# Attention, then two expert layers: six more tiles transposed by TensorE instead of by DMA

## The chip, the cores and the metric

The kernel runs on one core of one Trainium2 chip. The metric is the device time of one execution in microseconds, as the median of several runs. Five engines work side by side, each on its own queue of instructions in a fixed order: TensorE (PE; its weight loads are listed as PEld), VectorE (DVE), ScalarE (ACT), GpSimd (POOL) and SyncE (SP), which issues the transfers.

## The reference

```python
scores = np.matmul(q, k.transpose(0, 1, 3, 2)) / np.sqrt(D)   # q, k, v: 4 x 8 x 576 x 64
rel = np.abs(pos[:, None] - pos[None, :])
x = np.log1p(rel) / np.log1p(np.maximum(pos[:, None], 1.0))
bias = np.maximum(x[..., None] @ w1 + b1, 0.0) @ w2           # 32 hidden, 8 heads
scores = scores + bias.transpose(2, 0, 1)
attn = exp(scores - max) / (sum + 1e-9)
x = (attn @ v) as 2304 tokens x 512
h = max(x @ moe_w1, x @ moe_w2, x @ moe_w3)                   # 768 wide
x = h @ moe_w_out                                             # 512 wide
h = x @ moe2_w_in                                             # 2048 wide
g = h where h >= 1, 0 where h <= -1, else (h + 1)**2 / 4
out = g @ moe2_w_out
```

All arrays are float32. The kernel multiplies most matrices as pairs of float16 parts, a high and a low one, with three products for each pair of operands.

## The kernel before

The queries of a batch are cut into four blocks of 128 (j = 0 to 3) and a rest of 64. A **unit** is one block of one batch. The rest, called SJ (j = 4), packs two heads into one tile, so its unit has 4 **slots** where a long unit has 8, one for each head. Blocks 0 to 2 run over all four batches; then, batch by batch, block 3 and the rest follow, so the last two units are block 3 and the rest of batch 3: 8 and 4 slots, the last 12 of 144.

A slot goes like this. TensorE computes the scores in float32 (L632, in a PSUM tile s); VectorE adds the bias and takes the maximum (L644); ScalarE takes the exponential and its sum (L646), which leaves the tile pf (of the pool `sp`, 4 buffers). For the product with v (**PV**, L682 in the rest, L686 elsewhere), pf must be transposed and split into float16 parts. In most slots ScalarE writes the high part (L662), GpSimd the low part (L663 and L664) into a tile phl, and SyncE issues one DMA transpose (L666) of both into a tile pt (4 buffers). In every second slot of block 0 (j = 0) it is done otherwise: TensorE turns pf in float32 against an identity matrix (L651 four times 128 columns, L652 the last 64) into two tiles of the PSUM pool pm, ScalarE copies the high part out (L655, L656) and VectorE subtracts it for the low part (L657, L658). No DMA takes part. This is called a **set** below.

The pool pm has three buffers. They serve these sets, the products of the first layer (L741, 12 matmuls to a group) and of the second (L763, 18 to a group), and the small products that find the scale of a weight (L447). Groups are emptied by ScalarE (L746, L768) or VectorE (L748).

After the PV of a unit, VectorE divides by the sums (L698), ScalarE and GpSimd split (L700, L701), and a DMA transpose (L709) brings it to xT, which the first layer multiplies (L741), from work that is queued while later slots run. The first layer's result is split again (L752, L753) before L763, and L768 and L770 bring the result to DRAM.

Beside it run the **late pieces**, the 32 weight pieces of the last layers. Each is loaded (L416) in two 32-bit words, decoded by ScalarE (L428, L429) and VectorE (L430, L431), its scale found by L447, and split (L156, L157). Some land in the buffers of the tile v: two buffers, which also hold the v of a unit and half its heads, loaded by L601. When the last L741 and L763 are done, the last stage starts, which alternates L969 and L993.

What order each engine's instructions get is set by a scheduler that simulates times while the kernel is built; on the chip the order is fixed, and an instruction that waits holds up all behind it on its engine. This is true of SyncE's queue of transfers too.

```python
for j, b in [(j, b) for j in range(3) for b in range(B)] + [(j, b) for b in range(B) for j in (3, SJ)]:
```

Of the kernel before, what the change touches and what calls it, by code (L numbers as in the profile page):

```python
# [20 lines left out]
def kernel(ctx: ExitStack, tc: tile.TileContext, qt, kt, vr, small, mw1, mw2, mw3, mwo, win, wo2, out):  # L21
# [9 lines left out]
    B, H, S, D = 4, 8, 576, 64  # L31
# [60 lines left out]
    def st(shape, dt, tag):  # L92
        return sb.tile(shape, dt, tag=tag, name=tag, bufs=BUFS.get(tag, 1))
# [69 lines left out]
    if True:  # L163
# [61 lines left out]
        def mlp_ps():  # L225
            return ps.tile([P, 512], F32, tag="pm", name="pm", bufs=3)
# [343 lines left out]
        for j, b in [(j, b) for j in range(3) for b in range(B)] + [(j, b) for b in range(B) for j in (3, SJ)]:  # L570
            u = Unit()
# [62 lines left out]
        def halves(t):  # L634
            return t.rearrange("p (a c) -> p a c", a=2)

        def emit_soft(i):
            u, s = slots[i]
            if s == 0:
                u.sums = st([P, H], F32, "sums")  # L640
            h = s if u.j == SJ else HEADS[s]
            sn = st([P, S], F32, "sp")
            mx = st([P, 1], F32, "mx")
            V.tensor_tensor_reduce(halves(sn), sbox.pop(i)[:, :, :288], halves(bias_sb[u.j][:, h]), -0.125, 3e38, ALU.add, ALU.min, mx)  # L644
            pf = sn
            A.activation(pf, sn, AF.Exp, scale=-1.0, bias=mx, accum_out=u.sums[:, h:h + 1])  # L646
            if u.j == 0 and s % 2:

                pa, pe = mlp_ps(), mlp_ps()[0:64, :P]
                for c in range(4):  # L650
                    T.transpose(pa[:, P * c:P * c + P], pf[:, P * c:P * c + P], ident)  # L651
                T.transpose(pe, pf[:, 512:], ident)  # L652
                pt = st([P, 9, P], F16, "pt")
                pa = pa.rearrange("p (c i) -> p c i", c=4)
                A.activation(pt[:, 0:4], pa, AF.Copy)  # L655
                A.activation(pt[0:64, 4], pe, AF.Copy)  # L656
                V.tensor_tensor(pt[:, 5:9], pa, pt[:, 0:4], ALU.subtract)  # L657
                V.tensor_tensor(pt[64:128, 4], pe, pt[0:64, 4], ALU.subtract)  # L658
                ptbox[i] = pt
                return  # L660
            hl = st([P, 2 * S], F16, "phl")
            A.activation(hl[:, :S], pf, AF.Copy)  # L662
            G.tensor_tensor(hl[:, S:S + 64], pf[:, 512:], hl[:, 512:S], ALU.subtract)  # L663
            G.tensor_tensor(hl[:, S + 64:], pf[:, :512], hl[:, :512], ALU.subtract)  # L664
            pt = st([P, 9, P], F16, "pt")
            SP.dma_start_transpose(out=pt, in_=hl)  # L666
            ptbox[i] = pt
# [192 lines left out]
        for i in range(NS + LAG + 1):  # L860
            if i < NS:
                u, s = slots[i]
                at = i - start_of[u.j]
                if at == 0 and u.j < 3:
                    with behind(i):
                        new_xt(u.j + 1)
                    bias_q.extend((u.j + 1, gq) for gq in range(18))
                    if u.j == 2:
                        bias_q.extend((SJ, gq) for gq in range(9))
                with sooner("att"):  # L870
                    prefetch(i + PRM["ahead"])
                    prefetch_v(i)
                    emit_s(i + 1)
                    emit_soft(i)
# [199 lines left out]
```

## Time and profile before

| | |
|---|---|
| time, median of 3 runs | 1066.14 us (1061.78 to 1069.17) |
| the profiled execution | 1069.84 us, span 1068.1 us |
| TensorE busy | 969.3 us (91%) |
| VectorE busy | 688.4 us (64%) |
| ScalarE busy | 543.8 us (51%) |
| GpSimd busy | 310.2 us (29%) |
| mean granted clock of TensorE | 0.936 of full |
| the last scores L632 start | 575.0 us |

The page is of one execution, seen by the hardware profiler; its span is the time from the first to the last instruction. Busy shares are means over stages with different limits: TensorE is nearly full in most slices, while in the slices around 580 to 600 us it isn't. So the stretch from 545 to 600 us, in which the last twelve slots run, has to be read by itself.

### The profile page before, as it was taken

The numbers are of one execution on the slowest core, as the hardware profiler recorded it, in microseconds if no ns is written. First come the engines' busy times: TensorE is split into PE (matmuls) and PEld (weight loads), VectorE is DVE, ScalarE is ACT, GpSimd is POOL, SyncE is SP. The second block draws the span as 40 slices with busy tenths as digits, with TensorE's granted clock in tenths as the row PEclk, the third lists the DMA queues.
The fourth block names the chain that finished last, engine by engine and source line by source line (L and its number), as shares of the span: only waits on it lengthen the run. The fifth ranks groups of instructions, "written<-read, shape, count | busy, mean of one in ns | idle before, by whom it ended". The sixth has DMA issues, their size and how long they took to land.

```text
span 1068.1 us, 23316 instructions
## 1 busy us (share of the span) xinstructions
PE 969.3 (91%) x9218; PEld 671.4 (63%) x9218; DVE 688.4 (64%) x1614; ACT 543.8 (51%) x1104; POOL 310.2 (29%) x425
## 2 busy tenths in 40 slices
PE   6687879799999989999897788999999999999994
PEld 5555667678888878777686677644444444444562
DVE  8979877886555677456565598876654464454452
ACT  4486555676665645666666466543232332332341
POOL 1132234577767755556565112000000000000000
PEclk8676779899999989999999899999999999999997
DMA  9696767499999898989887745010110100000010
GB/s 299 198 284 172 181 152 159 119 216 201 241 231 210 188 181 156 192 218 224 186 180 182 211 153 164 21 40 1 40 40 1 40 21 1 7 34 1 4 38 20
DMA packets 229425, 138.94 MB, mean 130 GB/s; under 512 B 177988, under 2 KB 208196, under 8 KB 228804
## 3 DMA queue, kind: packets, MB, share of 16 engines
q1 hardware_dynamic: 229316, 137.45, 53.9%
q8 instruction: 72, 1.18, 0.5%
q14 instruction: 37, 0.30, 0.1%
HBM read 79.68 MB, written 15.27 MB: 89 GB/s over the span
## 4 chain that ended last, share of the span: by engine, by line
PE 63%; DMA 12%; DVE 12%; ACT 4%; issue 4%; SPq 2%; POOL 1%; DVEq 0%; POOLq 0%; ACTq 0%
PE pm L969 17%; PE s L993 17%; PE pm L741 11%; PE s L632 7%; PE pm L763 3%; PE pav L686 3%; DMA ws<-in_moe_w_out_dram 3%; DMA ws<-in_moe_w_in_dram 2%; PE pm L367 2%; DMA pt<-phl 2%; DVE sp L644 2%; DMA v<-in_moe_w_in_dram 2%; DMA aw<-in_moe_w_dram 1%; DVE aw L430 1%; DVE aw L157 1%
## 5 line engine op out<-in xcount | busy, mean ns | idle before, releaser
L741 PE MATMUL pm<-xT,aw 128*128 128x256 f16 (+1 forms) x2160 | 247.9, 268 | 19.6 <-ACT hm L746 4.9
L741 PEld LDWEIGHTS <-aw 128*128 128x128 f16 x2160 | 192.5, 100 | 59.9 <-issue 32.4
L664 POOL TENSOR_TENSOR phl<-sp,phl 128x512 f16<-128x512 f32 x128 | 154.2, 1205 | 0.1
L646 ACT ACTIVATE sp<-sp,mx 128x576 f32<-128x576 f32 x144 | 110.6, 769 | 84.1 <-DVE mx L644 83.8
L632 PE MATMUL s<-k,qz 64*128 64x288 f32 (+1 forms) x576 | 140.1, 475 | 10.6 <-DVE mx L644 9.7
L993 PEld LDWEIGHTS <-phl 128*128 128x128 f16 x864 | 84.5, 98 | 98.3 <-DVE phl L985 0.2
L981 DVE SCALAR_TENSOR_TENSOR sp<-pm,vec,sp 128x512 f32<-128x512 f32 (+1 forms) x80 | 55.8, 697 | 112.7 <-ACT sp L980 112.7
L980 ACT ACTIVATE sp<-pm,vec 128x512 f32<-128x512 f32 (+1 forms) x80 | 58.7, 733 | 123.8 <-PE pm L969 122.2
L993 PE MATMUL s<-ab,phl 128*128 128x512 f16 x486 | 112.5, 379 | 0.0
L984 ACT ACTIVATE phl<-sp,vec 128x512 f16<-128x512 f32 (+1 forms) x80 | 54.3, 678 | 109.4 <-DVE sp L982 109.4
L663 POOL TENSOR_TENSOR phl<-sp,phl 128x64 f16<-128x64 f32 x128 | 47.0, 367 | 205.9 <-ACT phl L662 152.6
L644 DVE CUSTOM_DVE_ANT_0 sp<-s,ab 128x576 f32<-128x576 f32 x128 | 93.1, 750 | 17.2 <-PE s L632 11.5
L632 PEld LDWEIGHTS s<-k,qz 64*128 64x128 f32 (+1 forms) x576 | 76.7, 207 | 36.4 <-DVE mx L644 13.9
L985 DVE SCALAR_TENSOR_TENSOR phl<-sp,vec,phl 128x512 f16<-128x512 f32 (+1 forms) x80 | 55.8, 698 | 51.7 <-ACT phl L984 51.6
L969 PEld LDWEIGHTS <-ab 128*128 128x128 f16 x540 | 52.7, 98 | 53.6
L686 PEld LDWEIGHTS <-pt 128*128 128x128 f16 x1792 | 73.5, 100 | 19.5 <-issue 7.8
L662 ACT ACTIVATE phl<-sp 128x576 f16<-128x576 f32 x128 | 84.0, 673 | 1.2 <-DMA pt<-phl 0.5
L763 PE MATMUL pm<-hh,wo 128*128 128x256 f16 x648 | 78.3, 276 | 5.7 <-ACT hh L752 3.5
L686 PE MATMUL pav<-v,pt 128*128 128x64 f16 x1568 | 70.3, 196 | 6.1 <-ACT pt L655 3.5
L763 PEld LDWEIGHTS <-wo 128*128 128x128 f16 x648 | 62.4, 99 | 13.4 <-issue 4.9
L753 POOL TENSOR_TENSOR hh<-hm,hh 128x256 f16<-128x256 f32 (+1 forms) x60 | 43.7, 728 | 92.5 <-ACT hh L752 92.5
L748 DVE SCALAR_TENSOR_TENSOR hm<-pm,hm 128x256 f32<-128x256 f32 (+1 forms) x120 | 46.9, 391 | 34.7 <-ACT hm L746 20.3
(213 smaller groups left out, 1445.8 us busy)
## 6 DMA issues: line engine op xcount, KB each, us to landing
k<-in_k_dram SPq DMA_DIRECT2D x64, 288.0 KB, 4.2
v<-v_d SPq DMA_DIRECT2D x24, 640.0 KB, 4.9
ws<-in_moe_w_out_dram SPq DMA_DIRECT2D x14, 512.0 KB, 4.5
x_d<-hl SPq DMA_DIRECT2D x36, 128.0 KB, 2.6
qz<-in_q_dram SPq DMA_DIRECT2D x16, 256.0 KB, 4.6
ab<-in_moe_w_dram SPq DMA_DIRECT2D x8, 512.0 KB, 8.5
ws<-in_moe_w_in_dram SPq DMA_DIRECT2D x8, 512.0 KB, 4.1
v<-in_moe_w_out_dram SPq DMA_DIRECT2D x8, 512.0 KB, 3.7
```

Source lines behind the costliest of these rows:

```text
L632: T.matmul(sbox[i + r][:, c, :288], q[p, s if u.j == SJ else s // 2], k[p, 288 * c:288 * c + 288], start=True, stop=True)
L644: V.tensor_tensor_reduce(halves(sn), sbox.pop(i)[:, :, :288], halves(bias_sb[u.j][:, h]), -0.125, 3e38, ALU.add, ALU.min, mx)
L646: A.activation(pf, sn, AF.Exp, scale=-1.0, bias=mx, accum_out=u.sums[:, h:h + 1])
L662: A.activation(hl[:, :S], pf, AF.Copy)
L664: G.tensor_tensor(hl[:, S + 64:], pf[:, :512], hl[:, :512], ALU.subtract)
L686: T.matmul(u.pav[:, 64 * h:64 * h + 64], pt[:, c], v[:, sl, 64 * (h % 4):64 * (h % 4) + 64], **kw)
L741: T.matmul(o, wm[:, ft, i, wp, kk], x_rhs(key, xp, kk) if n == 256 else x_rhs(key, xp, kk)[:, c], start=(x == 0), stop=(x == 11))
L763: T.matmul(pm, wo16[:, ft, wp, P * d:P * d + P], hh[:, ft, hp], start=(ft == 0 and y == 0), stop=(ft == NF1 - 1 and y == 2))
L969: T.matmul(pm, w[:, wp, kk], x2t[j][:, kk, xp], start=(x == 0), stop=(x == 11))
L980: A.activation(r, pm, AF.Relu, scale=c_ch[:, f], bias=c_half)
L981: V.scalar_tensor_tensor(t, pm, c_c[:, f], r, ALU.mult, ALU.max)
L993: T.matmul(acc[c], gl[:, n * gp + P * c:n * gp + P * c + P], w[:, wp], start=(start and y == 0), stop=(stop and y == 2))
```

## The change

The condition under which a slot takes the set of L651 to L658 in place of L662 to L666 is widened: from every second slot of block 0 to every second slot of the last two units also. These are the slots 1, 3, 5 and 7 of block 3 and 1 and 3 of the rest, in batch 3.

```diff
-            if u.j == 0 and s % 2:
+            if (u.j == 0 and s % 2) or (u.j >= 3 and u.b == B - 1 and s % 2):
 
                 pa, pe = mlp_ps(), mlp_ps()[0:64, :P]
                 for c in range(4):
                     T.transpose(pa[:, P * c:P * c + P], pf[:, P * c:P * c + P], ident)
                 T.transpose(pe, pf[:, 512:], ident)
                 pt = st([P, 9, P], F16, "pt")
                 pa = pa.rearrange("p (c i) -> p c i", c=4)
                 A.activation(pt[:, 0:4], pa, AF.Copy)
                 A.activation(pt[0:64, 4], pe, AF.Copy)
                 V.tensor_tensor(pt[:, 5:9], pa, pt[:, 0:4], ALU.subtract)
                 V.tensor_tensor(pt[64:128, 4], pe, pt[0:64, 4], ALU.subtract)
                 ptbox[i] = pt
                 return
             hl = st([P, 2 * S], F16, "phl")
             A.activation(hl[:, :S], pf, AF.Copy)
             G.tensor_tensor(hl[:, S:S + 64], pf[:, 512:], hl[:, 512:S], ALU.subtract)
             G.tensor_tensor(hl[:, S + 64:], pf[:, :512], hl[:, :512], ALU.subtract)
             pt = st([P, 9, P], F16, "pt")
             SP.dma_start_transpose(out=pt, in_=hl)
```

The scheduler then orders the stretch anew on every engine. On SyncE, before, this stood from the last late pieces that are loaded during the attention to the first one behind it. pt is a tile for PV, xT the layer's input, `x_d` the first part's result, `qz<-x_d` its way back, which waits for the last scores, and `v<-v_d` the last load of v.

```order
L416 DMA ws<-in_moe_w_out_dram 128x512
L666 DMA_TRANSPOSE pt<-phl 128x9x128 x4
L709 DMA_TRANSPOSE xT<-px 128x8x128
L786 DMA qz<-x_d_73 128x2048
L709 DMA_TRANSPOSE xT<-px 128x4x128
L601 DMA v<-v_d 128x2560
L770 DMA x_d_76<-hl 128x256 x3
L666 DMA_TRANSPOSE pt<-phl 128x9x128 x4
L416 DMA v<-in_moe_w_in_dram 128x4x128
L709 DMA_TRANSPOSE xT<-px 128x8x128
L770 DMA x_d_76<-hl 128x256
L416 DMA v<-in_moe_w_in_dram 128x4x128
```

The same place now:

```order
L416 DMA ws<-in_moe_w_out_dram 128x512
L666 DMA_TRANSPOSE pt<-phl 128x9x128 x2
L786 DMA qz<-x_d_73 128x2048
L601 DMA v<-v_d 128x2560
L709 DMA_TRANSPOSE xT<-px 128x8x128
L666 DMA_TRANSPOSE pt<-phl 128x9x128
L709 DMA_TRANSPOSE xT<-px 128x4x128
L770 DMA x_d_76<-hl 128x256
L666 DMA_TRANSPOSE pt<-phl 128x9x128
L770 DMA x_d_76<-hl 128x256
L709 DMA_TRANSPOSE xT<-px 128x8x128
L416 DMA v<-in_moe_w_in_dram 128x4x128
```

The load of v now stands ahead of both L709 that preceded it. Behind it there are two L666 where there were four in a row. The L709 of 8 rows that L741 waits for stands ahead of the weight load that it followed.

On ScalarE the place is the first decoding L428 of a late piece in the buffer of v, whose end lets SyncE issue the load of v. Before:

```order
L662 ACTIVATE phl<-sp 128x576
L752 ACTIVATE hh<-hm 128x256
L646 ACTIVATE sp,sums<-sp,mx 128x576
L700 ACTIVATE px<-xf 128x256
L662 ACTIVATE phl<-sp 128x576
L428 ACTIVATE sp<-v 128x512
L646 ACTIVATE sp,sums<-sp,mx 128x576
L662 ACTIVATE phl<-sp 128x576
L768 ACTIVATE hl<-pm,vec 128x128 x8
```

Now:

```order
L646 ACTIVATE sp,sums<-sp,mx 128x576
L746 ACTIVATE hm<-pm 128x256
L662 ACTIVATE phl<-sp 128x576
L655 ACTIVATE pt<-pm 128x512
L656 ACTIVATE pt<-pm 64x128
L428 ACTIVATE sp<-v 128x512
L646 ACTIVATE sp,sums<-sp,mx 128x576
L752 ACTIVATE hh<-hm 128x256
L768 ACTIVATE hl<-pm,vec 128x128 x2
L700 ACTIVATE px<-xf 128x256
L655 ACTIVATE pt<-pm 128x512
L656 ACTIVATE pt<-pm 64x128
```

L428 now follows the two copies of the set of slot 7, and the eight L768 that stood together are spread between the last two sets.

On TensorE the sets of the slots 1, 3 and 5 stand ahead of the last scores (L632), that of slot 7 right behind them, the two of the rest later. Two groups of 12 L741 and 15 matmuls of L763 that stood ahead of the last scores now stand behind them; the four groups of 18 L763 then stand: one ahead of the last PV of block 3, one within it and one after it, and the last behind the PV of the rest. Before, all four stood ahead of the PV of the slots 4 to 7.

## Rows read from the trace of the kernel before

**Rows 1.** Chain of waits, 571 to 600 us: start us, us, what.

```profile
577.99 5.06 DMA v<-v_d
...
589.27 3.36 DMA pt<-phl
...
593.67 5.20 DMA v<-in_moe_w_in_dram
```

**Rows 2.** TensorE's waits, 575 to 600 us: waiter, releaser: total us, times, longest.

```profile
PE pav L682 <- DMA pt<-phl: 5.2, 4, 2.8
```

**Rows 3.** TensorE's timeline: start us, us, instruction, count [idle before it, releaser].

```profile
563.57 1.47 PE L741 MATMUL pm<-xT,aw 128*128 128x256 f16 x12 [1.79 <-ACT hm L746]
...
574.26 1.14 PE L632 MATMUL s<-k,qz 128*128 128x288 f32 x4
575.23 6.39 PE L763 MATMUL pm<-hh,wo 128*128 128x256 f16 x57
...
583.09 1.79 PE L686 MATMUL pav<-v,pt 128*128 128x64 f16 x56 [1.24 <-DMA v<-v_d]
587.71 0.63 PE L682 MATMUL pav<-v,pt 128*64 128x64 f16 x28 [2.83 <-DMA pt<-phl]
...
591.30 0.96 PE L682 MATMUL pav<-v,pt 128*64 128x64 f16 x28 [0.54 <-DMA pt<-phl]
...
596.01 4.67 PE L741 MATMUL pm<-xT,aw 128*128 128x256 f16 x24 [2.38 <-DMA xT<-px]
...
600.75 2.78 PE L741 MATMUL pm<-xT,aw 128*128 128x256 f16 x24
603.37 0.39 PE L447 MATMUL pm<-ab,ones 128*128 128x128 bf16 x4
```

**Rows 4.** Windows: length; PE, PEld, DVE, ACT, POOL busy (count); granted clock, DMA share, GB/s.

```profile
190.00:200.00 10.00, 7.93 (x167) 7.41 (x165) 7.80 (x23) 4.96 (x12) 3.86 (x6) 1.00 0.24 70
...
545.00:596.00 51.00, 40.36 (x594) 33.80 (x592) 27.32 (x64) 28.90 (x64) 25.06 (x33) 0.94 0.84 185
...
586.00:588.00 2.00, 0.29 (x18) 0.29 (x20) 0.34 (x1) 0.34 (x1) 1.15 (x1) 1.00 0.57 120
...
590.00:592.00 2.00, 1.47 (x54) 1.33 (x52) 0.00 (x0) 0.00 (x0) 0.00 (x0) 0.50 1.05 200
...
596.00:680.00 84.00, 74.76 (x667) 63.64 (x668) 74.33 (x259) 54.27 (x114) 12.60 (x13) 0.96 0.47 149
```

**Rows 5.** TensorE's timeline in block 0, one set of the kind added.

```profile
197.79 0.61 PE L651 MATMUL pm<-ident,sp 128*128 128x128 f32 x4
198.23 0.27 PE L652 MATMUL pm<-ident,sp 128*64 128x128 f32 x1
```

**Rows 6.** Groups of instructions by form: count, busy us, mean ns, idle before.

```profile
L657 DVE TENSOR_TENSOR pt<-pm,pt 128x512 f16<-128x512 f32 x16 | 10.9, 682 | 2.7 <-ACT pt L655 2.7
...
L655 ACT ACTIVATE pt<-pm 128x512 f16<-128x512 f32 x16 | 9.3, 583 | 6.0 <-PE pm L651 5.9
...
L658 DVE TENSOR_TENSOR pt<-pm,pt 64x128 f16<-64x128 f32 x16 | 4.5, 284 | 0.5
...
L656 ACT ACTIVATE pt<-pm 64x128 f16<-64x128 f32 x16 | 4.2, 261 | 1.7 <-PE pm L652 1.7
```

**Rows 7.** Timelines of ScalarE and GpSimd, as in rows 3.

```profile
576.39 0.65 ACT L428 ACTIVATE sp<-v 128x512 f32<-128x512 f32 x1
...
586.42 1.15 POOL L701 TENSOR_TENSOR px<-xf,px 128x512 f16<-128x512 f32 x1 [5.96 <-ACT px L700]
```

**Rows 8.** Timeline of SyncE's queue: start and length of the issue.

```profile
590.80 0.47 SPq L416 DMA_DIRECT2D v<-in_moe_w_in_dram  x1
591.36 1.24 SPq L709 DMA_TRANSPOSE xT<-px  x1
```

**Rows 9.** Waits in block 0, 50 to 201 us: waiter, releaser: total us, times, longest.

```profile
PEld L686 <- ACT pt L655: 6.7, 3, 3.9
...
PE pm L741 <- DVE pt L658: 4.2, 2, 3.3
```

## The prediction

> **What bounds the kernel now.** I read the page's slices first, then the chain of waits, then TensorE's own waits and the busy windows around the end of the attention. Over most of the span TensorE is the bound; the changed slots are the last twelve of the attention, and they end where it is not. In the chain [rows 1] the reader is to see that the end is set there by transfers: the load of v (5.06 us), the landing of the last DMA transpose (3.36), a weight load (5.20). TensorE's waits in the same stretch are four for a transposed tile, 5.2 us in all [rows 2], and, in its timeline [rows 3], one for v before 583.09, 1.24, and one for xT before 596.01, 2.38: 8.9 us idle between 581.8 and 596.0. [...] In the 84 us behind it TensorE is busy 74.8 and VectorE 74.3 [rows 4]: neither has much slack, and both start from this place.
>
> **The change part by part.** Six of twelve slots (1, 3, 5 and 7 of the long unit, 1 and 3 of the short one) lose L662, L663, L664 and a DMA transpose, and get a set of L651, L652 and L655 to L658. One set holds TensorE from 197.79 to 198.50 us in the first block [rows 5]: 0.7, 4.2 for six. ScalarE's two copies are 0.58 and 0.26, VectorE's two subtractions 0.68 and 0.28 [rows 6], 5.0 and 5.8 us for six. Both engines are busy some 57% and 54% of 545 to 596 us [rows 4], so these sums hide as sums; GpSimd, at 25.1 of 51, only loses work, which ends nothing by itself. What counts is where TensorE and SyncE's queue then stand.
>
> (A) The last scores. TensorE has three sets more ahead of them, 3 x 0.7 = 2.1, but two groups of 12 L741 (24 hold it from 600.75 to 603.37, 2.6) and 15 L763 (57 take 6.39, so 1.7) now stand behind [rows 3]: 2.1 - 2.6 - 1.7 = -2.2. The stall of 1.79 us before 563.57 [rows 3], which ended with L746, I leave as it is, since that copy stays. The last scores ended at 574.26 + 1.14 = 575.4; now 573.2.
>
> (B) The load of v. Its buffer is freed by L428, at 576.39 before [rows 7], and SyncE issued the load at 577.99, behind the DMA transpose of a px tile. Now L428 stands behind the copies of slot 7: 573.2 + 0.7 + 0.58 + 0.26 + 0.65 = 575.4, and the px transpose has gone behind the load: issue at about 575.5 and, with the same 5.06, landing at 580.5, 2.5 earlier. Queued behind it on SyncE are that px transpose and the two DMA transposes left to the short unit, which need pt buffers that only the PV after v frees.
>
> (C) TensorE till then: one set, 24 L741, one set, 18 L763, 0.7 + 2.6 + 0.7 + 2.0 = 6.0 from 573.2, so 579.2. Each set holds two of the three pm buffers till ScalarE and VectorE have emptied them; a microsecond of such waits fits in before v binds.
>
> (D) From v to the end of the PV was 583.09 to 593.6, 10.5 us. Now 56 PV 1.8, two groups of 18 L763 between, 4.0, one set 0.7, and four PV of 28 at the full clock 4 x 0.63 = 2.5 [rows 3]: 9.0, end at 589.5, 4.1 earlier. The two DMA transposes land just in time: the first is freed at about 581 and lands some 3.4 later; the second has a px transpose (1.24 of issue) and a store (about as long as a load's 0.47) ahead of it [rows 8] and lands near 588, about when its PV could start.
>
> (E) The xT that L741 waited for. Before, its last step on GpSimd ended at 587.57 [rows 7], 2.7 after its PV (583.09 + 1.79). Now the PV end at 580.5 + 1.8 + 2.0 = 584.3; 2.7, and 0.84 for copies of a set that stand ahead on ScalarE, give 587.8, and the DMA as before from issue to use (591.36 [rows 8] to 596.01) 4.65: 592.4, 3.6 earlier. TensorE has its last L763 group in the meantime, which it had done long ago before.
>
> (F) The clock. TensorE would idle about 2 us between 575 and 592 where it idled 8.9, so I let it keep the full clock, and the 24 L741 give back another 1.9: 5.5 in all on TensorE. In the first block the granted clock over 190 to 200 us, with two such sets among dense matmuls, is 1.00 [rows 4]. [...]
>
> (G) What follows. The weight load at 593.67 [rows 1] waited for the last PV: 4.1 earlier. The one ahead of it, issued at 590.80 [rows 8], now stands behind the issue of xT, which ends near 589: 1.8 earlier only. So VectorE's decoding starts 1.8 to 4.1 earlier, 3.0 in the mean, and TensorE 5.5; with both nearly full afterwards I take the middle, **-4.3 us**. Ends for the range: 0, when VectorE decides and the new order of the later pieces costs the rest, and -9.7 (rival 1).
>
> The profiled execution's own 1069.84 becomes 1065.5. It lies 3.7 above the median of the runs shown (1066.14, from 1061.78 to 1069.17); the same change from there gives **1061.8**. About 1%, 10.7 us here, is what a measurement of this kernel can tell from no change, so this is a small gain below that.
>
> **The rivals.**
> (1) The whole tail closes. If all of the 8.9 goes, three PV at 0.96 us fall to 0.63 [rows 3] (1.0) and the 24 L741 by 1.9, that is 11.8, less the three sets behind the last scores, 2.1: -9.7, 1056.4. For it: the tail is all transfers [rows 1]. Against: the load of v is still one of them and only 2.5 earlier. Chance 0.15.
> (2) Given back. The tail gains, but the load that was at 590.80, and the decoding behind it, hold VectorE, busy 74.3 of 84 us: within 1.5 us of 1066.1. For it: VectorE's share, and the 1.8 of (G). Against: the loads behind are 4.1 earlier. Chance 0.17.
> (3) Slower, by the three pm buffers. In the first block TensorE stood twice with L741 for L658, 4.2 us, 3.3 at most, and its weight loads three times for L655, 6.7 us [rows 9]. If each of the three sets ahead of the last scores brings a wait of 2.1 (4.2 / 2), these end at 573.2 + 6.3 = 579.5, 4.1 later than before; the tail gives back 10.5 - 9.0 = 1.5, so +2.6: 1068.7. With such waits at all six, +8.9: 1075.0. It decides from about 3.7 us of waits ahead of the last scores (2.2 of (A) and 1.5). Against: VectorE was busy 78% of 190 to 200 us in that block and is 54% busy here [rows 4], and that block has 16 sets for the 10.9. Chance 0.10.
> (4) Slower, by the clock. Should the sets bring the lower clock from 573 to 592 us, some 14.5 us of TensorE work in it double, less the 4.3: +10, 1076. [...] Chance 0.03.
> That the change would not do what it says is excluded: the new order has six sets in place of six DMA transposes.
>
> **How the numbers follow.** The forecast has 0.55, the rivals 0.15, 0.17, 0.10 and 0.03. The range runs from rival 1, 1056.0, to a little over no change, 1067.5; outside lie the part of rival 1 beyond its price, most of rivals 3 and 4, and some of the spread of the runs. Faster by over 1% (below 1055.5) needs a little more than rival 1's full price: 0.07. Slower by over 1%: rival 4 and the far end of rival 3, 0.05. Within 1%: 0.88.
>
> **What would show it.** The last L632 ends near 573 us (A); the last load of v is issued near 575.5 (B); the last L682 ends near 589.5 (D); the first L741 on the last block's xT starts near 592 (E), at a granted clock of 1.00 (F); the first L969 starts some 4 us sooner than before (G). Wrong: waits of TensorE on L657, L658 or L746 above 3.7 us ahead of the last scores, a clock of 0.50 between 580 and 592, or an early L741 with L969 where it was.

## The result, and the profile after

The changed kernel takes 1070.57 us (median of 20 runs, 1066.58 to 1078.2) where the kernel before takes 1064.59 (20 runs, 1061.78 to 1072.92). The ratio is **1.0054, 95% interval 1.0037 to 1.0070**: about 5.8 us slower by the ratio, inside the 1% that one measurement can tell from no change, yet clear over many runs. The prediction was 4.3 us faster, with a range up to 1067.5. It has the wrong sign.

One execution starts this stretch some microseconds sooner or later than the next, also in one and the same order: the kernel before has the first L632 below at 543.80, and once more, held to its own order (e15), at 539.15. So all times are counted from an instruction that both kernels share: the first L632 of the last long unit's slots 0 and 1. TensorE's timelines, with columns as in [rows 3], first the kernel before, for that point and for the first L969, which begins the last stage:

```profile
543.80 1.24 PE L632 MATMUL s<-k,qz 64*128 64x288 f32 x8
...
679.65 10.09 PE L969 MATMUL pm<-ws,ab 128*128 128x512 f16 x46
```

The changed kernel, with the lines that answer to [rows 3]:

```profile
539.09 1.24 PE L632 MATMUL s<-k,qz 64*128 64x288 f32 x8
...
568.71 1.14 PE L632 MATMUL s<-k,qz 128*128 128x288 f32 x4
...
585.90 1.07 PE L682 MATMUL pav<-v,pt 128*64 128x64 f16 x56 [1.10 <-DMA pt<-phl]
586.91 2.14 PE L763 MATMUL pm<-hh,wo 128*128 128x256 f16 x18
588.89 0.39 PE L447 MATMUL pm<-ab,ones 128*128 128x128 bf16 x4
590.25 2.78 PE L741 MATMUL pm<-xT,aw 128*128 128x256 f16 x24 [0.97 <-PE pm L447]
594.04 0.39 PE L447 MATMUL pm<-ab,ones 128*128 128x128 bf16 x4 [1.01 <-ACT hl L768]
595.43 4.36 PE L741 MATMUL pm<-xT,aw 128*128 128x256 f16 x24 [0.99 <-ACT hm L746]
...
680.33 1.89 PE L969 MATMUL pm<-ws,ab 128*128 128x512 f16 x8
```

The changed kernel's times are 4.71 lower at the common point (543.80 - 539.09). So its first L741 on the last xT, at 590.25, stands against 596.01 [rows 3]: 51.2 us from the common point against 52.2, a gain of 1.0. Its first L969 stands at 141.2 against 135.9, a loss of 5.4; the rest to the end is 388.6 against 388.5. **The loss arises between the first L741 and the first L969**: 90.1 us against 83.6, in a stage whose code the diff does not touch.

Windows of the changed kernel (columns as in [rows 4]):

```profile
568.00:584.00 16.00, 14.37 (x177) 12.41 (x177) 8.21 (x20) 8.62 (x23) 4.82 (x7) 1.00 0.78 162
590.00:593.00 3.00, 2.75 (x24) 2.27 (x24) 0.04 (x1) 1.73 (x4) 0.67 (x1) 1.00 1.10 352
595.00:600.00 5.00, 4.57 (x30) 3.46 (x30) 3.90 (x11) 2.82 (x7) 0.50 (x1) 0.66 0.80 288
596.00:680.00 84.00, 69.49 (x632) 59.00 (x630) 71.90 (x256) 51.90 (x107) 13.07 (x12) 0.98 0.42 137
```

In the last one TensorE is busy 69.5 of 84 us and VectorE 71.9, both less than in [rows 4]. From the first L741 to the first L969 they have nearly the same work in both kernels, TensorE 74.4 and 73.6 us, VectorE 74.2 and 75.0, in 83.6 us before and 90.1 after. Neither was filled up; what grew is waiting, and something else paces them.

What that is, I read from SyncE's queue. Behind the PV the late pieces are loaded one by one (L416), and three raw buffers go round: load 6 takes the buffer that the decode of load 3 has freed. I call this the ring, the time from a load to the third one behind it a turn, and a place where the loads fall further behind those of the kernel before a slip. The kernel before, loads 3, 5, 6 and 7:

```profile
596.19 0.33 SPq L416 DMA_DIRECT2D v<-in_moe_w_out_dram  x1
...
600.13 0.33 SPq L416 DMA_DIRECT2D v<-in_moe_w_out_dram  x1
601.54 0.38 SPq L416 DMA_DIRECT2D v<-in_moe_w_in_dram  x1
608.26 0.33 SPq L416 DMA_DIRECT2D ws<-in_moe_w_out_dram  x1
```

The changed kernel, loads 1 and 2, the L709 of the short unit's px, then loads 3, 5, 6 and 7:

```profile
586.76 0.53 SPq L416 DMA_DIRECT2D v<-in_moe_w_in_dram  x1
...
587.96 1.27 SPq L416 DMA_DIRECT2D v<-in_moe_w_in_dram  x1
591.43 1.20 SPq L709 DMA_TRANSPOSE xT<-px  x1
592.95 0.34 SPq L416 DMA_DIRECT2D v<-in_moe_w_out_dram  x1
...
595.13 0.33 SPq L416 DMA_DIRECT2D v<-in_moe_w_out_dram  x1
600.78 0.38 SPq L416 DMA_DIRECT2D v<-in_moe_w_in_dram  x1
603.28 0.33 SPq L416 DMA_DIRECT2D ws<-in_moe_w_out_dram  x1
```

From load 3 to load 6 it is 5.3 us before and 7.8 after; load 3 itself is 1.5 later from the common point (53.9 against 52.4). Its buffer is freed by the decode of load 1, which leaves 0.7 later, lands after 4.9 us instead of 4.1, and is decoded at 592.92; the L709 ahead of load 3 has ended by then (591.43 + 1.20). Load 6 is then 4.0 late. Why, ScalarE's timeline shows. Before:

```profile
600.28 0.67 ACT L428 ACTIVATE sp<-v 128x512 f32<-128x512 f32 x1
600.84 0.68 ACT L429 ACTIVATE ab<-v 128x512 uint32<-128x512 uint32 x1
601.58 0.68 ACT L429 ACTIVATE ab<-ws 128x512 uint32<-128x512 uint32 x1
```

These are both halves of load 3's decode, then L429 of load 4; load 6 is issued 0.02 us behind the end of the second (600.84 + 0.68). After:

```profile
597.12 0.68 ACT L429 ACTIVATE ab<-v 128x512 uint32<-128x512 uint32 x1 [1.75 <-DMA v<-in_moe_w_out_dram]
597.69 0.71 ACT L156 ACTIVATE ab<-sp,vec 128x512 f16<-128x512 f32 x1
598.44 0.68 ACT L429 ACTIVATE ab<-ws 128x512 uint32<-128x512 uint32 x1
...
599.82 0.38 ACT L746 ACTIVATE hm<-pm 128x256 f32<-128x256 f32 x1 [0.40 <-PE pm L741]
600.10 0.66 ACT L428 ACTIVATE sp<-v 128x512 f32<-128x512 f32 x1
```

The L429 of load 3 runs as the weight lands, but its L428 stands three microseconds behind it, after L156, L429 of load 4, L752 and L746. It writes a tile of the pool `sp`, whose four buffers are taken in turn; this one was last held by the piece decoded ahead of load 1. I call that the **early piece**: its buffer is free only once VectorE's L157 has split it. VectorE before, its scale (L140) and split (L157):

```profile
582.59 0.15 DVE L140 TENSOR_SCALAR vec<-tcol 128x1 uint32<-128x1 uint32 x1
...
585.60 0.74 DVE L157 SCALAR_TENSOR_TENSOR ab<-sp,vec,ab 128x512 f16<-128x512 f32 x1
```

And after, from the maximum (L449) on:

```profile
589.32 0.29 DVE L449 TENSOR_REDUCE tcol<-pm 128x1 f32<-128x128 f32 x1 [1.80 <-PE pm L447]
592.96 0.69 DVE L430 SCALAR_TENSOR_TENSOR ab<-sp,ab 128x512 uint32<-128x512 uint32 x1 [3.35 <-ACT ab L429]
...
596.42 0.14 DVE L140 TENSOR_SCALAR vec<-tcol 128x1 uint32<-128x1 uint32 x1
...
598.59 0.74 DVE L157 SCALAR_TENSOR_TENSOR ab<-sp,vec,ab 128x512 f16<-128x512 f32 x1
```

From the common point the split starts at 41.8 before and at 59.5 after. The chain to it: pm buffers are taken in the order of the code. The last of the short unit's sets takes two of the three, so the last L763 groups come behind it, one of them behind the last PV (586.91), and the early piece's L447 behind that (588.89; before, it stood in the hole ahead of v, behind the L763 that end at 575.23 + 6.39 = 581.6 [rows 3]). It depends on the slot whether a set does this: alone in slot 3 (e13) it leaves the L447 ahead of the last PV, alone in slot 1 (e14) it does not. Then VectorE's scale stands behind L430 of load 1, for which VectorE idles 3.35 us, until load 1 has landed and ScalarE has decoded it. A second place of the kind lies some 30 us later, at loads 12 and 13. Loads 12, 13, 16 and 17 before, and after:

```profile
630.47 0.38 SPq L416 DMA_DIRECT2D v<-in_moe_w_in_dram  x1
635.01 0.33 SPq L416 DMA_DIRECT2D ws<-in_moe_w_out_dram  x1
...
644.57 0.38 SPq L416 DMA_DIRECT2D ws<-in_moe_w_in_dram  x1
650.43 0.33 SPq L416 DMA_DIRECT2D v<-in_moe_w_out_dram  x1
```

```profile
628.26 0.38 SPq L416 DMA_DIRECT2D v<-in_moe_w_in_dram  x1
635.26 0.33 SPq L770 DMA_DIRECT2D x_d<-hl  x1
635.82 0.33 SPq L416 DMA_DIRECT2D ws<-in_moe_w_out_dram  x1
...
641.89 1.36 SPq L416 DMA_DIRECT2D ws<-in_moe_w_in_dram  x1
651.09 0.33 SPq L416 DMA_DIRECT2D v<-in_moe_w_out_dram  x1
```

4.5 us from load 12 to 13 has become 7.6: a store, L770, now stands ahead of load 13 in the queue, and the L428 that frees its buffer stands behind the L429 of load 12, which waits for its landing, and two L768. ScalarE, after:

```profile
634.06 0.67 ACT L429 ACTIVATE ws<-v 128x512 uint32<-128x512 uint32 x1 [1.53 <-DMA v<-in_moe_w_in_dram]
...
635.13 0.67 ACT L428 ACTIVATE sp<-ws 128x512 f32<-128x512 f32 x1
```

The two slips do not simply add up. From the common point load 3 is 1.5 late and load 6 4.0, but load 7 is 0.3 early, and load 12 is 2.5 late. Load 13 is then 5.5 late, load 16 only 2.0, and load 17 5.4, as is the first L969. So in this one pair of executions 1.5 of the 5.4 us stands at load 3 already, the first slip has left 1.0 by load 12, and the second place has added the larger part, 2.9.

### The profile page after: what moved, and what is told of

Read it like the earlier page. It is cut to its first block, busy times and chain, and to the rows that moved or that the text cites. A ratio compares the mean times of both kernels' runs of the same rounds, so it can differ in the third digit from the quotient of the medians.

```text
span 1068.9 us, 23359 instructions
## 1 busy us (share of the span) xinstructions
PE 968.4 (91%) x9248; PEld 669.7 (63%) x9248; DVE 690.5 (65%) x1626; ACT 544.4 (51%) x1110; POOL 303.3 (28%) x413
## 4 chain that ended last, share of the span: by engine, by line
PE 63%; DVE 14%; DMA 9%; ACT 5%; issue 4%; POOL 2%; SPq 1%; DVEq 0%; POOLq 0%; ACTq 0%
PE pm L969 17%; PE s L993 17%; PE pm L741 11%; PE s L632 6%; PE pm L763 3%; DMA ws<-in_moe_w_out_dram 3%; PE pav L686 3%; DVE sp L644 2%; PE pm L367 2%; DMA ws<-in_moe_w_in_dram 2%; ACT sp L646 1%; DMA v<-in_moe_w_in_dram 1%; POOL phl L664 1%; DVE aw L430 1%; DVE aw L157 1%
## 5 line engine op out<-in xcount | busy, mean ns | idle before, releaser
L741 PE MATMUL pm<-xT,aw 128*128 128x256 f16 (+1 forms) x2160 | 245.6, 266 | 23.0 <-DVE hm L748 5.7
L741 PEld LDWEIGHTS <-aw 128*128 128x128 f16 x2160 | 190.9, 100 | 62.3 <-issue 37.6
L632 PE MATMUL s<-k,qz 64*128 64x288 f32 (+1 forms) x576 | 139.1, 468 | 11.8 <-DVE mx L644 9.3
L664 POOL TENSOR_TENSOR phl<-sp,phl 128x512 f16<-128x512 f32 x122 | 147.0, 1205 | 0.0
L993 PE MATMUL s<-ab,phl 128*128 128x512 f16 x486 | 112.5, 379 | 0.0
L984 ACT ACTIVATE phl<-sp,vec 128x512 f16<-128x512 f32 (+1 forms) x80 | 54.3, 679 | 109.4 <-DVE sp L982 109.4
L632 PEld LDWEIGHTS s<-k,qz 64*128 64x128 f32 (+1 forms) x576 | 75.9, 204 | 38.0 <-DVE mx L644 14.9
L985 DVE SCALAR_TENSOR_TENSOR phl<-sp,vec,phl 128x512 f16<-128x512 f32 (+1 forms) x80 | 55.8, 697 | 51.7 <-ACT phl L984 51.6
L969 PEld LDWEIGHTS <-ab 128*128 128x128 f16 x540 | 52.7, 98 | 53.6
L763 PE MATMUL pm<-hh,wo 128*128 128x256 f16 x648 | 77.7, 273 | 6.0 <-ACT hh L752 3.4
L662 ACT ACTIVATE phl<-sp 128x576 f16<-128x576 f32 x122 | 80.0, 671 | 1.4 <-DMA pt<-phl 0.7
L763 PEld LDWEIGHTS <-wo 128*128 128x128 f16 x648 | 61.7, 98 | 13.2 <-issue 5.7
```

The source lines that it names most:

```text
L632: T.matmul(sbox[i + r][:, c, :288], q[p, s if u.j == SJ else s // 2], k[p, 288 * c:288 * c + 288], start=True, stop=True)
L741: T.matmul(o, wm[:, ft, i, wp, kk], x_rhs(key, xp, kk) if n == 256 else x_rhs(key, xp, kk)[:, c], start=(x == 0), stop=(x == 11))
L763: T.matmul(pm, wo16[:, ft, wp, P * d:P * d + P], hh[:, ft, hp], start=(ft == 0 and y == 0), stop=(ft == NF1 - 1 and y == 2))
L969: T.matmul(pm, w[:, wp, kk], x2t[j][:, kk, xp], start=(x == 0), stop=(x == 11))
L985: V.scalar_tensor_tensor(gl[:, n:2 * n], t, c_ga[:, f], gl[:, :n], ALU.mult, ALU.subtract)
L993: T.matmul(acc[c], gl[:, n * gp + P * c:n * gp + P * c + P], w[:, wp], start=(start and y == 0), stop=(stop and y == 2))
```

## The experiments

Theory 1: the order of issue behind the attention loses the time. Theory 2: each set costs, by TensorE, the pm buffers or the clock. The others are named where they are tried. The table has the kernel before, the changed kernel and all 18 runs (12 executions each, but 6 of e4 and e12 and 10 of e9): the ratio to the kernel before, and, from one profiled execution of each, in us from the common L632: the first L741 on the last xT, load 3, the time from load 3 to 6, that from load 12 to 13, load 18, and the first L969.

| | ratio (95%) | L741 | load 3 | 3 to 6 | 12 to 13 | load 18 | L969 |
|---|---|---|---|---|---|---|---|
| before | 1 | 52.2 | 52.4 | 5.3 | 4.5 | 107.8 | 135.9 |
| changed | 1.0054 (1.0037-1.0070) | 51.2 | 53.9 | 7.8 | 7.6 | 113.2 | 141.2 |
| e1 long unit only | 1.0033 (1.0014-1.0051) | 55.0 | 55.3 | 5.2 | 4.3 | 112.5 | 139.5 |
| e2 short unit only | 1.0013 (0.9997-1.0029) | 47.6 | 50.6 | 8.6 | 7.4 | 108.4 | 136.9 |
| e3 changed, old order behind | 1.0008 (0.9991-1.0025) | 50.7 | 53.1 | 5.4 | 4.5 | 107.3 | 136.4 |
| e4 before, new order behind | 1.0049 (1.0031-1.0067) | 51.5 | 54.0 | 7.7 | 7.2 | 111.4 | 139.7 |
| e5 short only, old order behind | 0.9995 (0.9973-1.0016) | 47.0 | 50.5 | 5.7 | 4.5 | 105.5 | 133.6 |
| e6 before, new on DVE and ACT | 1.0049 (1.0025-1.0072) | 51.8 | 53.4 | 7.5 | 7.3 | 112.0 | 140.3 |
| e7 before, new on DVE | 1.0019 (0.9996-1.0043) | 51.2 | 51.3 | 5.9 | 5.2 | 106.8 | 136.6 |
| e8 before, new on SP | 1.0055 (1.0035-1.0075) | 52.0 | 55.3 | 6.2 | 7.0 | 113.9 | 141.4 |
| e9 changed, early piece early | 1.0041 (1.0016-1.0066) | 49.0 | 51.9 | 5.6 | 7.3 | 108.5 | 136.9 |
| e10 the same, one L428 more | 1.0026 (1.0007-1.0046) | 51.1 | 53.8 | 5.3 | 7.0 | 109.2 | 137.6 |
| e11 short only, the same moves | 1.0023 (1.0003-1.0043) | 47.9 | 52.1 | 5.7 | 7.2 | 109.6 | 137.8 |
| e12 before, early piece late | 1.0066 (1.0042-1.0089) | 51.7 | 51.7 | 9.1 | 4.5 | 109.5 | 136.9 |
| e13 slot 3 only | 0.9994 (0.9974-1.0014) | 49.3 | 52.5 | 5.7 | 3.6 | 106.3 | 134.6 |
| e14 slot 1 only | 0.9967 (0.9950-0.9984) | 47.2 | 51.3 | 5.0 | 3.5 | 105.4 | 132.6 |
| e15 before, own order held | 1.0003 (0.9976-1.0030) | 52.1 | 52.2 | 5.4 | 4.5 | 106.8 | 134.7 |
| e16 as e12, again | 1.0025 (1.0001-1.0049) | 54.1 | 54.1 | 9.0 | 4.5 | 112.3 | 140.2 |
| e17 slot 1, old order behind | 0.9997 (0.9980-1.0015) | 47.3 | 50.5 | 5.9 | 4.5 | 106.9 | 135.0 |
| e18 slot 1 only, again | 0.9992 (0.9965-1.0019) | 50.6 | 54.3 | 5.0 | 3.5 | 108.6 | 135.6 |

Down the last two columns: **the first L969 comes 27.0 to 29.8 us behind load 18 in every one of them**, while load 18 itself moves by 8.5 us (105.4 to 113.9). It follows the first L741 only in part: e2, e5, e14 and e17 start 4.6 to 5.2 us early and end between 1.0 later and 3.2 sooner than the kernel before. I read from this that the ring of loads sets the end of the stage. The steady distance alone would not show it, since whatever comes so late in the stage could keep step with its end; e8 and e12 below are the test: one changes the order of SyncE's queue alone, the other seven instructions of the decoding.

**Which slots (e1, e2).**

```diff
-            if (u.j == 0 and s % 2) or (u.j >= 3 and u.b == B - 1 and s % 2):
+            if (u.j == 0 and s % 2) or (u.j == 3 and u.b == B - 1 and s % 2):   # e1; e2: u.j == 4
```

> Only the long unit's four slots are changed, the short unit keeps its DMA transposes. Behind the last PV TensorE then has the order of the kernel before, without a difference. Theory 1 (the loss of the change lies in the order in which the work behind the attention is issued, and this order is pushed over by the short unit's sets): 0.998 to 1.001 times before, that is -2 to +1 us. Theory 2 (each set of transposes costs, by TensorE, the pm buffers or the clock, whatever the order): four sixths of +5.7 us, +3.8 us, 1.0036.

> Only the short unit's two slots are changed, the long unit keeps its DMA transposes. Behind the last PV every engine then has the order of the changed kernel, without a difference. Theory 1 (order behind the attention): the full loss with two sets alone, +4.5 to +7 us, 1.004 to 1.0065. Theory 2 (a price for each set): two sixths of +5.7 us, +1.9 us, 1.0018.

1.0033 and 1.0013: both outside theory 1's ranges, and by the ratios alone theory 2's numbers. The profile says otherwise. e1 has neither slip; its first loads come 2 to 3 us late. On SyncE two stores stand there between the short unit's four L666, which stood in a row before; that these stores are e1's loss was not tested. e2 has both slips of the changed kernel, but starts 4.6 us early. By the profiles the two halves agree with theory 2 by cancelling, not by its reason; that the sets as such cost little is shown by e3.

**The order behind the last PV (e3, e4).** In these and all later kernels with an order put in from outside, every instruction gets a dependence without a semaphore on the one that is to precede it on its engine, from a table:

```diff
+        if _e in _last:
+            tc.add_manual_dep(_i, _last[_e].name, mybir.DependencyInfo(mybir.DependencyClass.NoSync, mybir.DependencyReason.DATA), reason="order")
+        _last[_e] = _i
```

> The changed kernel with all six sets, but everything behind the last PV is issued on every engine in the order of the kernel before; one group of 18 L763, which the changed order has behind the last PV, stands first there. Theory 1 (order behind the attention): the loss is gone, 0.998 to 1.002. Theory 2 (price of the sets): the loss stays, 1.004 to 1.007. Theory 3 (the group of 18 L763, pushed behind the last PV by the short unit's second set in the sequence of the pm buffers, delays the start of that stage): 2.0 us of TensorE and its eviction stay, 1.002 to 1.004.

> The kernel before, with no set in the late slots, but everything behind the last PV is issued on every engine in the order of the changed kernel (the last group of L763 stays ahead of the PV, where the kernel before has it). Theory 1 (order behind the attention): slower by +4 to +6.5 us, 1.004 to 1.006, without any transposition by TensorE. Theory 2 (price of the sets) and theory 3 (the L763 group behind the PV): 0.998 to 1.001.

Here theory 1 holds in both directions. All six sets in the old order cost 0.8 in a thousand, not told from nothing; no set in the new order costs 4.9. e4's TensorE has the kernel before's order but for two matmuls of L763 that change places with two of L447, so it isn't TensorE's order. Theory 3, the L763 group as such, is seen in e3's stage, which takes 85.8 us for 83.6, about the 2.0 of those 18 matmuls; but it starts 1.5 sooner, and little is left. e15 holds the kernel before to its own order and shows what holding costs:

> Control: the kernel before with every engine held to the very order that it has anyway. All theories: 0.998 to 1.002. Its profiled execution is a second one of the kernel before: first L741 on the last xT 52.2 us and first L969 135.9 us behind the first L632 of the last long unit's slots 0 and 1 there; I expect both within 1 us, should one execution of this stage be like the next.

1.0003, and the stage 82.7 us for 83.6: one execution is like the next to about 1 us.

**Which engine's order (e6, e7, e8, with the orders of these engines alone exchanged behind the last PV).**

> The kernel before; behind the last PV only VectorE and ScalarE have the order of the changed kernel, TensorE, GpSimd and SyncE keep the old one. With all engines in the new order the run was 1.0049. Theory 6 (the two engines that decode the late weights and empty the pm buffers: in the new order decodes stand ahead of evictions): 1.0035 to 1.005. Theory 7 (SyncE: in the new order the last px transpose stands ahead of weight loads): 0.999 to 1.001.

> The kernel before; behind the last PV only VectorE has the order of the changed kernel. Theory 6 with VectorE as the one that decides: as with VectorE and ScalarE together, 1.0035 to 1.005. Theory 6 with ScalarE as the one that decides: 0.999 to 1.0015. Theory 7 (SyncE): 0.999 to 1.001.

> The kernel before; behind the last PV only SyncE and GpSimd have the order of the changed kernel: SyncE issues the last px transpose two weight loads sooner, and one store of x2 two loads later; GpSimd's order is the same in both. Theory 7 (SyncE): 1.0025 to 1.005. Theory 6 (VectorE and ScalarE): 0.999 to 1.001.

Neither theory 6 nor 7 is alone right: ScalarE with VectorE gives the whole loss (1.0049), SyncE by itself too (1.0055), and all together (e4, 1.0049) no more. VectorE alone is between, with an interval that holds no change; ScalarE alone was not run. I read them as different doors into the same ring. In e8 the L709 stands ahead of loads 3 and 4, which come 2.9 us late (55.3 against 52.4), with the decodes in their old order; in e6 load 3 is 1.0 late, and the turn from 3 to 6 takes 7.5 us.

**One piece (e9, e10, e12, e16).** Theory 8, which the second text below sets out, is the chain told above for the early piece. The edit of e12 on ScalarE, with VectorE's L135, L136, L140 and L157 of the early piece put behind L430 of load 1 to match; load 3's weight is what the texts call the weight three pieces on:

```diff
-L156 (early piece)
 L428, L429 (load 1)
 ...
-L428 (load 3)
 L429 (load 3)
+L156 (early piece)
 L429 (load 4)
 L752, L429, L746
+L428 (load 3)
```

e9 does the reverse in the changed kernel, with the last group's two L768 ahead of L700 besides. e10 also moves the L428 that frees load 13's buffer ahead of the L429 and the two L768 at the second place.

> The kernel before in its own order, with no set in the late slots; only the scale and split of the first late piece and the L428 of the weight three pieces on are put as late as the changed kernel has them (seven instructions, and one L430 that follows from it). Theory 8: the load that waits for that L428 comes 3 to 4 us later and the run is 2.5 to 4.5 us slower, 1.0025 to 1.0045. Any theory in which this piece is covered by other work: 0.999 to 1.001.

> The changed kernel in its own order, but for nine instructions behind the last PV: the two L768 of the last L763 group stand ahead of the last L700 on ScalarE, the scale and split (L135, L136, L140, L156, L157) of the late piece whose sum is formed first stand ahead of the decode of the next piece, and the L428 of the weight three pieces on stands ahead of its L429. Theory 8 (the sets' pm buffers push that piece's sum behind the last PV; its sp buffer then comes free late, the L428 that needs it is late, and with it the raw buffer and the load that waits for it, 4.0 us later than in the kernel before, 1.4 us after the load ahead of it there and 5.7 in the changed kernel): that load 2.5 to 3.5 us sooner, the whole 2 to 4 us sooner than the changed kernel, 1.0015 to 1.0035. Theory 2 (price of the sets, 1.0054) or an order that loses everywhere a little: 1.0045 to 1.006.

> As the run before, and one instruction more: the L428 of the late weight that in the changed kernel stands behind two L768 and a L429 that waits for a landing is put ahead of them (there the second load was 3.0 us later against the load ahead of it than in the kernel before). Theory 8 with a second slip of the same kind: 1 to 2.5 us less than the run before, 1.000 to 1.002. Theory 8 with the first slip alone: as the run before.

> The kernel before with the first late piece's split and the L428 three pieces on put late, a second time. Theory 8: 1.0025 to 1.0045, with the first L969 2 to 5 us later than in the kernel before, counted from the common L632. Should the first profile be typical (1.0 us later) and its times not: 1.000 to 1.002. Should the order change something ahead of the stage: the common L632 itself comes later than elsewhere.

e12, ScalarE's two moved instructions and then loads 3 and 6:

```profile
599.79 0.72 ACT L156 ACTIVATE ab<-sp,vec 128x512 f16<-128x512 f32 x1
...
603.63 0.66 ACT L428 ACTIVATE sp<-v 128x512 f32<-128x512 f32 x1
```

```profile
595.16 0.33 SPq L416 DMA_DIRECT2D v<-in_moe_w_out_dram  x1
...
604.31 0.38 SPq L416 DMA_DIRECT2D v<-in_moe_w_in_dram  x1
```

Load 6 leaves as that L428 ends, 9.1 us behind load 3 where it was 5.3: 3.8 later, where 3 to 4 was expected, from seven moved instructions (the text above counts one too many), with no set in the late slots; the second place stays at 4.5. In e12 load 3 is 0.7 early and load 18 1.7 late, in e16 1.8 and 4.5 late: of the slip 2.4 and 2.7 us are left at load 18. In time it is 1.0066, and 1.0025 the second time; the first above the 1.0025 to 1.0045 expected and the second at its lower end; the two differ by more than I can explain (the profiled executions put the first L969 1.0 and 4.3 us later). In e9 and e10 the turn from 3 to 6 is back at 5.6 and 5.3 us. e10 starts the stage within 0.1 us of the changed kernel and ends it 3.6 sooner (137.6, 141.2); its time gives back about half of the loss (1.0026), e9's a quarter (1.0041), with intervals that overlap the changed kernel's. Both lie above what theory 8 gave them (1.0015 to 1.0035, and 1.000 to 1.002): the first slip is part of the loss, and I put the rest down to the second place, where both runs stay at 7.0 and more; no run closes that place by itself. The second move of e10 hardly helped (7.0 for 7.3), and SyncE's queue shows why:

```profile
633.97 0.33 SPq L770 DMA_DIRECT2D x_d<-hl  x1
634.35 0.42 SPq L416 DMA_DIRECT2D ws<-in_moe_w_out_dram  x1
```

The L428 ended at 632.6 there (631.95 and 0.67), but load 13 stands behind the store, which waits for L768 (633.33 and 0.62, so 633.95). That moving the store as well would close the second slip was not tried.

**Is there a gain to be had (e5, e11, e13, e14, e17, e18)?** With e2's early start in the old order, with e9's moves, and with a single set:

```diff
-            if (u.j == 0 and s % 2) or (u.j >= 3 and u.b == B - 1 and s % 2):
+            if (u.j == 0 and s % 2) or (u.j == 4 and u.b == B - 1 and s == 3):   # e13; e14, e18: s == 1
```

> Only the short unit's two slots are changed, and everything behind the last PV is issued in the order of the kernel before (the last group of 18 L763, which this version has behind the last PV, stands first there). In the run with the short unit alone, the first L741 on the last block's xT came 4.6 us sooner than before, measured from a common matmul of the long unit, and the stretch from it to the first L969 took 89.3 us in the new order; in the old order this stretch took 83.6 (before) and 85.8 (all sets, old order). Theory 1 (the start and the order add up, each by itself): the first L969 2.4 to 4.6 us sooner than before, 0.9955 to 0.998. Theory 5 (the stage's end is set by the weight loads and VectorE, so that an earlier start is given back in the old order as well): 0.999 to 1.001.

> The kernel with the short unit's two sets alone, in its own order, with the same ten instructions moved. Its first L741 on the last xT came 4.6 us sooner than before and its stage took 5.7 us longer. Theory 8: the stage is 3 to 5 us shorter, so 2 to 4 us below the kernel before, 0.996 to 0.998. Theory 2 or an order that loses everywhere: as without the moves, 1.001 to 1.0015.

> Only slot 3 of the short unit is changed (one set). The sum of the first late piece keeps its place ahead of the last PV, no L763 stands behind it, and the L428 of the weight three pieces on stands ahead of its L429, as in the kernel before. Theory 8: no slip at the load that waits for that L428 (1 to 2.5 us after the load ahead of it), and the start of the stage 0.5 to 2.5 us sooner by the one DMA transpose less: 0.997 to 1.000. Theory 2 (price of a set, 5.7 / 6): 1.0009. A new order that loses at large: 1.003 or more.

> Only slot 1 of the short unit is changed (one set). The sum of the first late piece now stands behind the last PV, with three L763, but the L428 of the weight three pieces on stays ahead of its L429. Theory 8: the load that waits for it slips by 1 to 3 us, the start of the stage comes 0.5 to 2.5 us sooner: 0.999 to 1.002, and in any case more than with slot 3 alone. Theory 2: 1.0009. A new order that loses at large: 1.003 or more.

> One set in slot 1 of the short unit, and everything behind the last PV in the order of the kernel before (three L763 that this version has behind the last PV stand first there). Theory 8: no slip at the load that waits for the L428 three pieces on, the stage 82.5 to 85 us instead of 85.5, the start as with slot 1 alone: 0.5 to 3 us less than that, 0.994 to 0.9965. If the start and the order do not add (the stage's end is bound elsewhere): as slot 1 alone, 0.996 to 0.999.

> The kernel with one set in slot 1 of the short unit, a second time: 0.995 to 0.9985; if the first measurement was a lucky one, 0.9985 to 1.001.

e5 starts 5.2 us early and keeps 2.3 at the first L969; its time is 0.9995. Theory 5 is nearer than theory 1: an early start is mostly given back, since load 3 comes only 1.9 earlier. e11 failed: the turn from 3 to 6 is 2.9 us shorter than in e2, but load 3 came 1.5 later (load 1 took 6.0 us to land for 4.9), and from load 6 to 7 it took 5.3 us for 2.5, which gave the rest back; why it did is not settled. e13 came about as expected, without a slip. e14 did better than I said and had no slip either (2.4 us from load 5 to 6, where I expected the sum's place to cost 1 to 3): by these two, what counts is L428 standing ahead of L429, not the sum's place by itself. Its 0.9967 was not seen again (e18, 0.9992), nor did the old order add to it (e17, 0.9997, where theory 8 had 0.994 to 0.9965). No version is shown to beat the kernel before.

## Why the prediction was wrong

The steps, in the time of the kernel before (the changed kernel's plus 4.71):

| step | before | predicted | measured |
|---|---|---|---|
| (A) last scores end | 575.4 | 573.2 | 574.6 |
| (B) issue of the last v; landing | 577.99; 583.05 | 575.5; 580.5 | 576.7; 582.1 |
| (D) end of the PV | 593.6 | 589.5 | 591.7 |
| (E) first L741 on the last xT | 596.01 | 592.4 | 595.0 |
| (G) loads 1 and 2 | 590.80; 593.67 | 1.8 and 4.1 earlier | 0.7 later; 1.0 earlier |
| (G) first L969 | 679.65 | about 4 earlier | 5.4 later |

**The step that failed is (G).** I took the stage behind as paced by TensorE and VectorE, because both are nearly full there [rows 4], and passed on the middle of their two earlier starts. It is paced by loads whose buffers turn round, and each turn goes through ScalarE's and SyncE's fixed order: with the new order behind the last PV put into the kernel before (e4) the time is 1.0049, and with the old order in the changed kernel (e3) 1.0008. I had cited that stage's new order only as "costs the rest" at the zero end of the range, with nothing below it, though the rows to price it by were there: the weight load of 5.20 us that the chain ran through [rows 1]. A stage whose order the scheduler writes anew needed an end on the slow side.

**(A) to (E)** had the right sign; what was measured is 0.3 to 0.5 of the size. v took 5.46 us instead of 5.06. (C) and (E) placed the last L763 group behind the PV, at no cost to TensorE. That is so, but I did not ask what stood behind that group in the sequence of the pm buffers: the early piece's sum, and with it the chain above. The L741 at 590.25 is put down to that sum's buffer, but ScalarE's L700 waits for the same xT until 590.25 too, 4.83 us behind its issue (585.42), as (E) had it with 4.65; the issue itself was later than I thought, behind a PV end that was.

**(F)** was right where it looked. The granted clock is 1.00 from 568 to 584 us, with three sets in it, and at 590 to 593, and the 24 L741 there take 2.78 instead of 4.67 [rows 3]. But the next 24 take 4.36, in a window at 0.66, behind waits of 1.01 and 0.99 us for L768 and L746: 1.9 gained and 1.6 lost. That idle time ahead of them brings the lower clock was my estimate, from the 0.50 at 590 to 592 us before [rows 4]; the 0.66 agrees with it, but no run tries it alone. The 1.00 over 568 to 584 us shows no fall that goes with the sets.

**The rivals.** (1), the whole tail closing (1056.4 by its own sum, 1056.0 in the range), did not come. (2), given back, had the place (the loads and the decoding behind them) but not the size, and VectorE was not what decided: it is less busy than before, 71.9 us of 84 for 74.3 [rows 4]. (3) had the buffers, by the wrong way: between 543 and 600 us TensorE waits for a set twice, 0.4 us ahead of the last scores and 0.3 behind, for L657, and ahead of the last scores 0.5 us for L746, far from 3.7; the pm buffers cost by the order in which they are taken. (4), the lower clock, is out: 1.00 from 568 to 584 us, where it was to fall, and 0.98 in the 84 us behind. No row had shown that the sets would bring it, and its doubling of TensorE's work was an estimate; what was measured is 4.36 us for 24 L741 at 0.66, against 2.78 at 1.00. That the transposes themselves cost little is shown by e3.

That an instruction which waits holds up those behind it on its engine can be read here from VectorE: it idles 3.35 us ahead of 592.96, for the landing and decode of load 1, while the early piece's scale, ready since 589.6 (589.32 + 0.29), stands behind it.

## What to carry to other kernels

Where a scheduler writes the order, an edit is also a new order for all that follows; read what paces the next stage (here a ring of three raw buffers) and where its instructions now stand, before passing a gain on. A buffer taken in the order of the code ties together work that has nothing else in common: two more of a pool of three moved a small sum 12 us back, past the PV, and with it one load by 4 and those that followed by up to 2.7. A late load is not yet a late stage: follow the lateness to the end, and see where it is made good and where it comes back. And a dose test can fit a wrong theory: four of the six sets gave 61% of the loss and the other two 24%, and by the profiles these were two unlike effects, told apart only by counting from a common instruction.

## What had not been expected

The new orders of VectorE with ScalarE, and of SyncE, each by itself in the old kernel, cost as much as both (1.0049, 1.0055, and 1.0049 together). And 5 us gained at the start of a stage in which TensorE is busy 89% were worth, without a slip, 0.9 to 3.2 us at its end (e17 135.0, e14 132.6, against 135.9). What stays open is the difference between the two measurements of the same kernel in e12 and e16, and in e14 and e18; the profiled stage differs by about 1 us between executions of one order, the start of it by up to 3.5 (47.2 and 50.6).
